# Keys first, identity turns during the loads, and an earlier place on ScalarE for two units' exponentials: one core of a Trainium2

## The chip, the cores and the metric

The kernel runs on one core of one Trainium2 chip. The metric is the device time of one execution in microseconds (us), and of several executions the median is taken. Everything is 32-bit float. The engines are named as in the profile: PE is TensorE's matmul, PEld its weight load, DVE is VectorE, ACT is ScalarE, POOL is GpSimd, SP is SyncE, which only issues DMAs here. ACT issues DMAs too, so there are two DMA queues.

## What is computed

```python
scores = (q @ k.T) / 8                      # 8 batch rows, 8 heads, 576 tokens, 64 wide
thresh = max(scores, axis=-1) - tau
scores = where(scores >= thresh, scores, -1e9)
attn   = exp(scores - max(scores))
attn   = attn / (sum(attn) + 1e-9)
x      = attn @ v                           # heads side by side: (8, 576, 512)
h      = relu(x.T @ w_tok1) @ w_tok2        # mixes the tokens, 576 -> 256 -> 576
u      = x + h.T
out    = u + relu(u @ w_ch1) @ w_ch2        # mixes the channels, 512 -> 1536 -> 512
```

The weights come as 64-bit floats and are turned into 32-bit floats on the chip.

## The kernel before

The work is cut into 144 units, 18 for each batch row. A unit is 128 query tokens of one pair of heads (one unit in nine shares its tokens between two pairs). The program order is written out by hand: one loop over `u` emits, for each `u`, the scores of unit `u` and the later steps of earlier units, and every engine runs its own instructions in the order in which they were emitted. The steps that matter here are these.

- `load_qk` loads one pair of heads. Queries (`lq`) and keys (`lk`) arrive in eight parts, four of queries (even numbers) and four of keys (odd numbers), each 32 columns wide; a list of two queues says which engine issues queries and which issues keys. For pair 0 the first 128 query tokens were loaded ahead of the other 448.
- `prep` turns the loaded blocks into `qT` and `kT` with DVE transposes (L286).
- `scores` (L304) puts the scores of a unit into two PSUM tiles `sc`, one for each head of the pair; DVE takes their maximum `mx` (L309), POOL makes the `bias` of it (L310). There are two `sc` tiles, and a third in row 0.
- `weigh` is ACT's part: two Prelu instructions (L319) read `sc` and write `e`, which frees the PSUM tiles for the next unit's scores, and two exponentials (L326) work in place on `e`. For two heads it is one block of four large instructions.
- `norm` divides `e` by its sum (DVE L333 and L334, POOL L337).
- `turn` is used in batch row 0 only. It transposes a unit's `e` on PE in three thirds of three 128x128 blocks (L355) into the PSUM tiles `tr`, of which there are two. The first and the last third are copied out by DVE and the middle third by ACT (all L357). From row 1 on `turn_blocks` does this with DVE and DMAs (L367). Turns run two units behind: units 16 and 17, row 0's last, are turned while units 18 and 19, row 1's first, are scored.
- `weight(n)` emits the next `n` steps of the conversion of the weights. A weight piece passes through ACT (L197, L199), DVE (L207, L209, L213) and POOL (L221), and L207 of a piece reads what L199 wrote.
- `fill` emits matmuls of the token and channel layers while the attention of later rows runs.
- `tau` is loaded by one small DMA on ACT's queue, and five DVE instructions of one column each (L620 to L624) make `toff` and `ntau` of it.

`weigh(u)` stood near the end of the loop body, behind `turn` and `weight`. In row 0 it was moved ahead of them in the iterations in which a group's values fall due (`visit`). In the two iterations that have a row-0 unit to turn while a row-1 unit is scored (`turns_left` is true, `u` = 18 and 19) it stood behind them.

A DMA issue waits, besides for its data, for the landing of an earlier DMA that used the same one of eight landing semaphores; the eight are handed out in turn.

Of the kernel before, what the change touches and what calls it, by code (L numbers as in the profile page):

```python
# [9 lines left out]
F32 = mybir.dt.float32  # L10
# [7 lines left out]
P = 128  # L18
# [3 lines left out]
def kernel(  # L22
# [25 lines left out]
    nc = tc.nc  # L48
    B, H, S, D = q.shape
# [5 lines left out]
    MAIN = NI * P  # L55
# [14 lines left out]
    work = ctx.enter_context(tc.tile_pool(name="work", bufs=2))  # L70
    small = ctx.enter_context(tc.tile_pool(name="small", bufs=6))
    ps_sc = ctx.enter_context(tc.tile_pool(name="ps_sc", bufs=2, space=bass.MemoryType.PSUM))
    ps_tr = ctx.enter_context(tc.tile_pool(name="ps_tr", bufs=2, space=bass.MemoryType.PSUM))
# [17 lines left out]
    loaded = {}  # L91
# [3 lines left out]
    def load_qk(n, eng, parts=range(8), blocks=(range(S // 32),) * 2):  # L95


        b, p = pairs[n]
        if n not in loaded:
            loaded[n] = [ld.tile([P, S // 32, 32], F32, tag=tag, bufs=1, name=f"{tag}_{n}") for tag in ("lq", "lk")]  # L100
        for part in parts:
            i, which = divmod(part, 2)
            h, c = divmod(i, 2)
            lo, hi = blocks[which].start, blocks[which].stop
            eng[which].dma_start(
                out=loaded[n][which][32 * i : 32 * i + 32, lo:hi],
                in_=(q, k)[which][b, 2 * p + h, 32 * lo : 32 * hi, 32 * c : 32 * c + 32].rearrange("(n t) d -> t n d", t=32),
            )
# [9 lines left out]
    ident = const.tile([P, P], F32, name="ident")  # L118
# [1 line left out]
    for t in vlast:  # L120
        nc.gpsimd.memset(t, 0.0)

    load_qk(0, (nc.sync, nc.scalar), blocks=(range(P // 32), range(S // 32)))
    load_qk(0, (nc.sync, None), range(0, 8, 2), blocks=(range(P // 32, S // 32), None))
    nc.scalar.dma_start(out=tau_sb, in_=bass.AP(tensor=tau.tensor, offset=0, ap=[[0, P], [1, 1]]))

    w1 = const.tile([P, NT, DTOK], F32, name="w1")
# [143 lines left out]
    heads = {}  # L271
# [5 lines left out]
    def in_blocks(b):  # L277
        return b > 0

    def prep(n, first=S // 32):  # L280

        srcs = loaded.pop(n)
        heads[n] = [work.tile([P, S], F32, tag=name, name=f"{name}_{n}") for name in ("qT", "kT")]
        for which, lo, hi in ((0, 0, first), (1, 0, S // 32), (0, first, S // 32)):
            if lo < hi:
                nc.vector.transpose(  # L286
                    out=heads[n][which][:, 32 * lo : 32 * hi], in_=srcs[which][:, lo:hi].rearrange("p n d -> p (n d)")
                )

    def scores(u):  # L290
        b, p0, t = units[u]
        sc = [
            (ps_3rd if b == 0 and (2 * u + h) % 3 == 2 else ps_sc).tile([P, 2, MAIN], F32, tag="sc", name=f"sc{h}_{u}") for h in range(2)
        ]
        if t == SHARED:
            parts = [(b * NP + p0, slice(MAIN, S), slice(0, 64)), (b * NP + p0 + 1, slice(0, LAST), slice(64, P))]
        else:
            o = P * t if t < SHARED else LAST + P * (t - SHARED - 1)
            parts = [(b * NP + p0 + (t > SHARED), slice(o, o + P), slice(0, P))]
        order = [(f, part, h) for f in range(2) for part in parts for h in range(2)]  # L300
        for f, (n, cols, rows), h in order if b else sorted(order, key=lambda o: o[2]):
            r = slice(D * h, D * h + D)
            qT, kT = heads[n]
            nc.tensor.matmul(sc[h][rows, f, 0:HS], lhsT=qT[r, cols], rhs=kT[r, HS * f : HS * f + HS], start=True, stop=True)  # L304
        mx = small.tile([P, 2], F32, tag="mx", name=f"mx_{u}")
        bias = small.tile([P, 2], F32, tag="bias", name=f"bias_{u}")
        for h in range(2):
            c = slice(h, h + 1)
            nc.vector.tensor_reduce(out=mx[:, c], in_=sc[h][:, :, 0:HS], axis=AX.XY, op=ALU.max)  # L309
            nc.gpsimd.tensor_scalar(out=bias[:, c], in0=mx[:, c], scalar1=toff, scalar2=-SCALE, op0=ALU.add, op1=ALU.mult)  # L310
        st[u] = sc, bias

    def weigh(u):
        sc, bias = st.pop(u)
        rs = small.tile([P, 2], F32, tag="rs", name=f"rs_{u}")
        e = work.tile([P, 2 * S], F32, tag="e", bufs=3, name=f"e_{u}")
        for h in range(2):
            eh = e[:, S * h : S * h + S].rearrange("p (f x) -> p f x", f=2)
            nc.scalar.activation(out=eh, in_=sc[h][:, :, 0:HS], func=AF.Prelu, bias=bias[:, h : h + 1], scale=SCALE, alpha=STEEP)  # L319
        st[u] = e, rs  # L320

        if b_now:
            fill(0.2)
        for h in range(2):
            eh = e[:, S * h : S * h + S]
            nc.scalar.activation(out=eh, in_=eh, func=AF.Exp, bias=ntau, accum_out=rs[:, h : h + 1])  # L326
            if b_now:
                fill(0.2)
# [259 lines left out]
    def fill(share):  # L588
        nonlocal credit
        credit += share * quota  # L590
        while todo and credit > 0:
            cost, step = todo.popleft()
            credit -= cost
            step()
        if not todo:
            credit = 0.0
# [19 lines left out]
            todo.extend(channel_mlp(b - b % 2, uT, i))  # L616
        quota = (sum(c for c, _ in todo) - (KEEP if b else KEEP_FIRST)) / (UB - 1)

    prep(0, P // 32)
    nc.vector.tensor_scalar(out=tlow, in0=tau_sb, scalar1=0.0, scalar2=-3.0e38, op0=ALU.is_lt, op1=ALU.mult)  # L620
    nc.vector.tensor_scalar(out=toff, in0=tau_sb, scalar1=0.0, scalar2=FAR, op0=ALU.max, op1=ALU.min)
    nc.vector.tensor_scalar(out=toff, in0=toff, scalar1=-1.0 / SCALE, scalar2=None, op0=ALU.mult)
    nc.vector.tensor_add(out=toff, in0=toff, in1=tlow)
    nc.vector.tensor_scalar(out=ntau, in0=toff, scalar1=SCALE, scalar2=None, op0=ALU.mult)  # L624
    due = deque()
    b_now = 0
    LAG = 2
# [13 lines left out]
    for u in range(len(units) + LAG + 4):  # L641
        on = u < len(units)
        if u == UB:
            late.close()
            ps_mm = ctx.enter_context(tc.tile_pool(name="ps_mm", bufs=2, space=bass.MemoryType.PSUM))
        if on:
            b_now, p0, t = units[u]
            n = b_now * NP + p0
        w = u - LAG
        back = 0 <= w < len(units)  # L650
        if on:
            scores(u)

        last = False
        visit = False
        if due and not in_blocks(due[0][1]):
            visit = due[0][0] <= u
            last = values_due(u)
        elif early:
            early.popleft()[1]()  # L660
        if 0 < u <= len(units):
            norm(u - 1)

        turns_left = b_now and back and not in_blocks(units[w][0])
        if b_now:
            if not turns_left:
                weight(2)
        else:


            weight_to(2.25 * (u - (1 if visit else 1.5)))
            if visit and on:
                weigh(u)
        while copies:
            copies.popleft()()
        if last and u < UB:
            early.extend(token_mlp(0, range(NP // 2))[0])
        elif last:
            push(0)
        if back:  # L680
            wb, wp, wt = units[w]
            if not in_blocks(wb):
                for i in range(3):
                    turn(w, i)
            if wt % GU == GU - 1:
                g = wt // GU
                if g < 2:
                    split_middle(wb * NP + wp + g)
                due.append((u + (2 if in_blocks(wb) else 1), wb, wp, g))
        if b_now:  # L690
            fill(0.4)
        if back and in_blocks(wb):
            turn_blocks(w)
        if b_now:
            weight(4 if turns_left else 2)
        if on and (b_now or not visit):
            weigh(u)
        elif b_now:
            fill(0.6)
        if b_now:  # L700
            weight(2)
        elif u == 0:
            on_scalar(0, 0)
            on_scalar(0, 1)
        else:
            weight_to(2.25 * (u - 1))
        if on:


            when = {3: (2, 0, 2), 4: (2, 2, 4), 5: (2, 4, 6), 6: (2, 6, 8), 8: (3, 0, 3), 0: (1, 3, 6), 1: (1, 6, 8)}  # L710
            if u == 0:
                load_qk(1, (nc.sync, nc.sync), range(0, 3))
            if t in when:
                m, lo, hi = when[t]
                if n + m < len(pairs):
                    load_qk(n + m, (nc.scalar if b_now else nc.sync,) * 2, range(lo, hi))
            if t in (3, 7) and n + 2 + t // 4 < len(pairs):
                load_v(n + 2 + t // 4)
            if t == 2:
                prep(n + 1)  # L720
            if t == 7 and n + 2 < len(pairs):
                prep(n + 2)
        if due and in_blocks(due[0][1]):
            values_due(u)

        if back and wt % GU == 0 or not on:
            move_u()
# [31 lines left out]
```

## Time and profile before

| | |
|---|---|
| median of 5 runs | 1354.25 us (1353.75 to 1356.04) |
| the profiled execution | 1354.09 us, of which its span is 1352.3 us |
| PE busy | 1304.9 us, 96% of the span |
| DVE, ACT, POOL busy | 44%, 43%, 26% |
| mean granted PE clock | 0.991 |
| first score matmul | 6.91 us into the span |
| first maximum (DVE L309) | 9.23 us |
| first Prelu (ACT L319) | 10.47 us |
| row 1's first unit scored | 98.87 us |

A profile line of the timeline reads: start in us, duration in us, engine, line, operation, what it writes `<-` what it reads, shapes, `xcount` of merged instructions, and in brackets how long its engine sat idle before it and what ended that. A line of the chain of work that ended last reads: start, length, what. A line of the table by stages gives, for a stretch `A:B`, its length, then each engine's busy time with the count of its instructions, then the granted PE clock (1 is full speed), the share of time in which the DMA engines were busy, and GB/s.

### The profile page before, as it was taken

The page shows a single profiled execution, that of the slowest core. Times are in us where ns is not written, and L with a number is a line of the kernel's source. Part 1 is how long each engine was busy: PE and PEld are TensorE (multiplying, and loading weights), DVE is VectorE, ACT ScalarE, POOL GpSimd, SP SyncE. Part 2 cuts the span into 40 slices and gives each one's busy share as a digit, 9 for nine tenths or more (in the row PEclk, how much of TensorE's full clock was granted, in tenths as well). Part 3 has the DMA queues.
Part 4 walks back from the last instruction along what each step waited for, and adds up shares of the span by engine and source line. Part 5 has one row for each costly group of instructions (what it writes and reads, how often), then busy time and mean ns, then how long its engine had stood idle before and what let it go on. Part 6 is the DMA issues. An engine that isn't in the chain of part 4 may idle for free.

```text
span 1352.3 us, 17840 instructions
## 1 busy us (share of the span) xinstructions
PE 1304.9 (96%) x6162; PEld 812.0 (60%) x6162; DVE 592.7 (44%) x1026; ACT 585.2 (43%) x1299; POOL 354.6 (26%) x683
## 2 busy tenths in 40 slices
PE   6888899999999999999999999999999999999999
PEld 4555656547474666565665567465657466575677
DVE  6878874435443444434344444435443454201000
ACT  6776664444444444443434444344434453120110
POOL 4565652222222222212122222222221222100000
PEclk8998999999999999999999999999999999999999
DMA  5434764545354444443445435534443453400000
GB/s 123 117 88 121 203 167 96 126 95 130 89 130 97 105 108 105 121 108 87 92 102 125 104 78 128 127 81 110 114 102 82 113 119 78 112 24 17 23 24 32
DMA packets 296746, 135.31 MB, mean 100 GB/s; under 512 B 204816, under 2 KB 289552, under 8 KB 296656
## 3 DMA queue, kind: packets, MB, share of 16 engines
q1 hardware_dynamic: 168048, 118.16, 34.4%
q10 hardware_dynamic: 128608, 16.01, 7.5%
q8 instruction: 49, 0.80, 0.2%
q14 instruction: 41, 0.34, 0.1%
HBM read 43.25 MB, written 9.44 MB: 39 GB/s over the span
## 4 chain that ended last, share of the span: by engine, by line
PE 89%; DVE 5%; ACT 2%; DMA 2%; issue 1%; POOL 1%; SPq 0%; ACTq 0%; DVEq 0%; POOLq 0%
PE c L528 27%; PE c L507 27%; PE sc L304 12%; PE pv L416 9%; PE t L454 5%; PE t L464 4%; PE pv L411 3%; DVE mx L309 2%; PE tx L447 1%; ACT e L319 1%; PE tr L355 1%; PE c_h L555 1%; DMA lk<-in_k_dram 1%; DMA lq<-in_q_dram 1%; ACT e L326 0%
## 5 line engine op out<-in xcount | busy, mean ns | idle before, releaser
L507 PE MATMUL c<-xT,wc 128*128 128x256 f32 (+1 forms) x1920 | 400.2, 362 | 0.1
L309 DVE TENSOR_REDUCE mx<-sc 128x1 f32<-128x576 f32 x288 | 204.2, 750 | 446.7 <-PE sc L304 446.7
L528 PE MATMUL c<-wc,g 128*128 128x512 f32 x840 | 379.0, 597 | 0.0
L507 PEld LDWEIGHTS c<-xT,wc 128*128 128x128 f32 x1920 | 334.5, 191 | 69.8 <-issue 29.7
L310 POOL TENSOR_SCALAR bias<-mx,toff 128x1 f32<-128x1 f32 x288 | 82.6, 287 | 775.6 <-DVE mx L309 720.9
L319 ACT ACTIVATE e<-sc,bias 128x576 f32<-128x576 f32 x288 | 199.8, 740 | 179.3 <-POOL bias L310 174.6
L528 PEld LDWEIGHTS c<-wc,g 128*128 128x128 f32 x840 | 154.4, 190 | 176.3 <-issue 172.9
L326 ACT ACTIVATE e<-e,ntau 128x576 f32<-128x576 f32 x288 | 221.1, 772 | 0.0
L337 POOL TENSOR_SCALAR e<-e,rr 128x576 f32<-128x576 f32 x288 | 214.7, 758 | 14.3 <-ACT g L508 2.6
L508 ACT ACTIVATE g<-c 128x256 f32<-128x256 f32 (+1 forms) x240 | 86.9, 362 | 297.0 <-PE c L507 273.4
L304 PE MATMUL sc<-kT,qT 64*128 64x288 f32 (+1 forms) x1280 | 192.5, 434 | 12.7 <-DVE kT L286 6.9
L367 DVE STREAM_TRANSPOSE T<-e 128x1152 f32<-128x1152 f32 x126 | 171.9, 1364 | 4.8 <-DMA eT<-T 2.6
L304 PEld LDWEIGHTS sc<-kT,qT 64*128 64x128 f32 (+1 forms) x1280 | 106.4, 178 | 98.7 <-issue 56.7
L416 PE MATMUL pv<-eT,lv 128*64 128x384 f32 (+1 forms) x1024 | 137.5, 409 | 0.0
L416 PEld LDWEIGHTS pv<-eT,lv 128*64 128x64 f32 x1024 | 75.5, 138 | 50.8 <-issue 42.5
L421 ACT COPY xT<-pv 128x384 f32<-128x384 f32 (+1 forms) x56 | 21.0, 400 | 166.8 <-PE pv L416 163.8
L464 PE MATMUL t<-w,a 128*128 128x288 f32 x256 | 75.1, 420 | 8.2 <-DVE xT L468 4.8
L540 DVE TENSOR_TENSOR us<-c,ut 128x512 f32<-128x512 f32 x26 | 17.9, 690 | 137.5 <-PE c L528 120.4
L454 PE MATMUL t<-x_sb,w 128*128 128x512 f32 (+1 forms) x180 | 73.6, 557 | 0.0
L464 PEld LDWEIGHTS t<-w,a 128*128 128x128 f32 x256 | 45.8, 191 | 30.3 <-issue 10.5
L468 DVE TENSOR_TENSOR xT<-xT,t 128x288 f32<-128x288 f32 x64 | 28.3, 446 | 71.1 <-PE t L464 70.6
L326 ACT ACTIVATION_READ_ACCUMULATOR e<-e,ntau 128x1 f32 x288 | 56.6, 197 | 0.0
(49 smaller groups left out, 562.6 us busy)
## 6 DMA issues: line engine op xcount, KB each, us to landing
eT<-T SPq DMA_DIRECT2D x672, 108.0 KB, 2.3
scratch<-in_moe_w_ch_dram SPq DMA_DIRECT2D x24, 512.0 KB, 3.7
lv<-in_v_dram SPq DMA_DIRECT2D x32, 288.0 KB, 3.3
out_dram<-us SPq DMA_DIRECT2D x35, 256.0 KB, 2.2
lk<-in_k_dram ACTq DMA_DIRECT2D x111, 72.0 KB, 2.6
lq<-in_q_dram ACTq DMA_DIRECT2D x106, 72.0 KB, 2.3
ut<-us SPq DMA_DIRECT2D x192, 32.0 KB, 1.9
lq<-in_q_dram SPq DMA_DIRECT2D x18, 72.0 KB, 3.4
```

The source lines that it names most:

```text
L304: nc.tensor.matmul(sc[h][rows, f, 0:HS], lhsT=qT[r, cols], rhs=kT[r, HS * f : HS * f + HS], start=True, stop=True)
L309: nc.vector.tensor_reduce(out=mx[:, c], in_=sc[h][:, :, 0:HS], axis=AX.XY, op=ALU.max)
L319: nc.scalar.activation(out=eh, in_=sc[h][:, :, 0:HS], func=AF.Prelu, bias=bias[:, h : h + 1], scale=SCALE, alpha=STEEP)
L326: nc.scalar.activation(out=eh, in_=eh, func=AF.Exp, bias=ntau, accum_out=rs[:, h : h + 1])
L337: nc.gpsimd.tensor_scalar(out=eh, in0=eh, scalar1=rr[:, h : h + 1], scalar2=1.0, op0=ALU.mult, op1=ALU.mult)
L367: nc.vector.transpose(out=T[:, :, place, :].rearrange("p a (c x) -> p c a x", c=NK), in_=e.rearrange("p (c a x) -> p c a x", c=NK, a=4))
L416: nc.tensor.matmul(to[r], lhsT=lv[:, j, :], rhs=e[j], start=False, stop=(c == NI - 1), skip_group_check=True)
L454: nc.tensor.matmul(to, lhsT=w1[:, t, P * m : P * m + P], rhs=x_sb[:, t, cols], start=(t == 0), stop=(t == NT - 1))
L464: nc.tensor.matmul(to, lhsT=a[:, m, P * c : P * c + P], rhs=w2[:, m, HS * f : HS * f + HS], start=(m == 0), stop=(m == NTK - 1))
L507: nc.tensor.matmul(ps, lhsT=wc1[:, j, c, :], rhs=uT[:, c, GR * i : GR * i + n], start=(c == 0), stop=(c == NCC - 1))
L508: nc.scalar.activation(out=s["g"][:, j, 0:n], in_=ps, func=AF.Relu)
L528: nc.tensor.matmul(flat, lhsT=s["g"][:, j, P * t : P * t + P], rhs=wc2[:, j, :], start=(j == 0 and b > 0), stop=(j == NJ - 1), skip_group_ ...
```

## The change

There are three edits.

1. The first loads. The four parts of the keys of pair 0 are now issued first, two by SP and two by ACT; then the four first parts of its queries (128 tokens), two by each; then, as before, SP alone issues the other 448 query tokens. `tau` stays behind them on ACT's queue. DVE's order at the start becomes: keys' transpose, first queries' transpose, the five `tau` instructions, the other queries' transpose. Before it was: first queries, keys, other queries, `tau`.
2. 24 PE transposes of the identity into a `tr` tile that nobody reads stand ahead of the first score matmul.
3. At `u` = 18 and 19 `weigh(u)` is emitted ahead of `turn` and `weight`. On ACT these two units' Prelus and exponentials come to stand ahead of the copy of the turn's middle third and ahead of one L197/L199 pair. The `fill` calls there have nothing to emit yet. PE, POOL and the later part of every other engine's order stay the same.

```diff
-    load_qk(0, (nc.sync, nc.scalar), blocks=(range(P // 32), range(S // 32)))
-    load_qk(0, (nc.sync, None), range(0, 8, 2), blocks=(range(P // 32, S // 32), None))
+    FIRST = P // 32
+    for which in (1, 0):
+        for i in range(2):
+            for eng, half in ((nc.sync, 0), (nc.scalar, 1)):
+                load_qk(0, (eng, eng), [2 * (2 * half + i) + which], (range(FIRST), range(S // 32)))
+    load_qk(0, (nc.sync, None), range(0, 8, 2), (range(FIRST, S // 32), None))
...
-    prep(0, P // 32)
+    warm = ps_tr.tile([P, MAIN], F32, tag="tr", name="warm")
+    for _ in range(24):
+        nc.tensor.transpose(out=warm[:, 0:P], in_=ident, identity=ident)
+    prep(0, ((1, 0, S // 32), (0, 0, FIRST)))
     nc.vector.tensor_scalar(out=tlow, in0=tau_sb, ...)
...
+    prep(0, ((0, FIRST, S // 32),))
...
         turns_left = b_now and back and not in_blocks(units[w][0])
         if b_now:
-            if not turns_left:
+            if turns_left:
+                weigh(u)
+            else:
                 weight(2)
         else:
             weight_to(2.25 * (u - (1 if visit else 1.5)))
-            if visit and on:
+            if visit:
                 weigh(u)
...
         if b_now:
             weight(4 if turns_left else 2)
-        if on and (b_now or not visit):
+        if turns_left:
+            fill(0.6)
+        elif on and (b_now or not visit):
             weigh(u)
```

`prep` takes the list of pieces to transpose in place of one number; for all later pairs it emits what it did before.

More of the change, by code (lines that the diff above doesn't have):

```diff
@@ L278, in in_blocks, with prep @@
         return b > 0
[L280 to L288, printed above, removed]
+    def prep(n, parts=((0, 0, S // 32), (1, 0, S // 32))):
+        if n not in heads:
+            heads[n] = [work.tile([P, S], F32, tag=name, name=f"{name}_{n}") for name in ("qT", "kT")]
+        for which, lo, hi in parts:
+            nc.vector.transpose(
+                out=heads[n][which][:, 32 * lo : 32 * hi], in_=loaded[n][which][:, lo:hi].rearrange("p n d -> p (n d)")
+            )
     def scores(u):
```

## The prediction

> **What bounds the kernel now.** I read the page's chain of work first, to see what a microsecond saved at the start is worth.
>
> ```profile
> PE 89%; DVE 5%; ACT 2%; DMA 2%; issue 1%; POOL 1%; SPq 0%; ACTq 0%; DVEq 0%; POOLq 0%
> ```
>
> PE is 89% of it; the rest is where other engines or loads hold PE up. The change touches only two such places, 0 to 24 us and 98 to 124 us. Behind each lies PE work of fixed amount, so a gain or loss there should reach the end whole. The chain from 0 to 24 us, its longest pieces:
>
> ```profile
> 1.17 2.07 DMA lq<-in_q_dram
> 3.27 2.73 DMA lk<-in_k_dram
> 6.07 0.79 DVE kT L286
> 6.91 2.30 PE sc L304 x8
> 9.23 0.77 DVE mx L309
> 10.47 1.37 ACT e L319 x2
> 11.85 1.51 ACT e L326 x4
> ...
> 15.13 2.29 PE sc L304 x4
> 17.41 1.49 PE tr L355 x6
> 19.45 0.92 PE tr L355 x3
> ```
>
> The keys' last part is issued only at 3.27, when a queries' part has landed, and lands at 6.00. Then come kT, unit 0's scores, maximum, Prelu and exponentials, each waiting for the one before. Now the same stretch by the clock:
>
> ```profile
> 6.90:11.00 4.10, 4.09 (x12) 2.54 (x12) 2.63 (x8) 0.53 (x1) 0.52 (x2) 1.00 1.07 347
> 14.00:17.50 3.50, 2.37 (x5) 1.32 (x6) 0.46 (x2) 3.22 (x7) 1.63 (x3) 0.52 0.81 129
> 17.50:21.00 3.50, 2.93 (x13) 2.07 (x15) 2.34 (x7) 2.08 (x4) 1.99 (x3) 0.50 0.01 1
> 21.00:24.40 3.40, 3.06 (x14) 1.76 (x10) 3.37 (x8) 2.60 (x7) 0.54 (x2) 0.50 0.00 0
> 24.40:28.00 3.60, 2.63 (x25) 1.74 (x25) 3.60 (x7) 3.60 (x9) 3.60 (x5) 1.00 0.00 0
> ```
>
> The clock is at half from 14 to 24 us. The 1.00 of the first row can't be right: eight score matmuls take 2.30 us at 6.91, and 1.24 us at 36.05 (`36.05 1.24 PE sc L304 x8` in the chain), so unit 0 ran at half speed too. Last, the second place, from the timelines of ACT and DVE:
>
> ```profile
> 104.14 0.39 ACT L456 ACTIVATE a<-t 128x256 f32<-128x256 f32 x1 [5.09 <-PE t L454]
> 104.80 0.48 ACT L357 COPY eT<-tr 128x384 f32<-128x384 f32 x1 [0.27 <-PE tr L355]
> 106.28 1.36 ACT L319 ACTIVATE e<-sc,bias 128x576 f32<-128x576 f32 x2
> ```
> ```profile
> 107.67 0.42 DVE L207 TENSOR_SCALAR high<-high 128x512 f32<-128x512 f32 x1
> 108.12 1.39 DVE L209 TENSOR_SCALAR wc<-high 128x512 uint32<-128x512 uint32 x1
> 110.16 1.42 DVE L309 TENSOR_REDUCE mx<-sc 128x1 f32<-128x576 f32 x2
> ```
>
> Unit 18's Prelus start at 106.28, though their bias was there at 102.46 and ACT was idle until 104.14. But the chain there runs through DVE: L207, L209, L213, then unit 19's maximum.
>
> **Keys first.** Issues on a queue stand 0.48 us apart at the start (SP's eight in 3.85 us). Two keys' parts on each queue are issued at 0.73 and 1.2, the queries' firsts at 1.65 and 2.1, none of them behind a landing. Parts of keys took 2.1 to 2.7 us to land, so they land at 2.8 to 3.9; queries' firsts took 2.0, so 4.1. kT (0.78) and the first of qT (0.31) then end near 5.0. Before, kT ended at 6.85: PE's data are ready 1.9 us earlier. The queries' rest and the first weight piece go out some 0.4 us later on SP; that piece, 5.4 us from issue to landing, would be there near 10.4, and ACT's L197 needs it only at 13.25, or about 12 after this change, so it costs nothing.
>
> **The turns of the identity.** At half clock six turns take 1.54 us (17.34) and three 0.90 (19.45): (1.54 - 0.90) / 3 = 0.213 us each. At full clock 0.87 (26.39) and 0.55 (28.08): 0.107 each. The identity is ready at 1.30, so 24 turns end between 1.35 + 24 x 0.107 = 3.9 and 1.35 + 24 x 0.213 = 6.5. PE is in order, so unit 0's scores start at 5.0 at best and 6.5 at worst. With 1.24 or 2.30 us each they end between 6.3 and 8.8, against 9.21.
> Whether turns raise the clock: in the row 21.00:24.40 PE is busy 3.06 us, of which 1.54 are six turns, and the clock then rises; in 14.00:17.50, with 2.37 us busy and nearly all of that scores, it didn't. So turns seem to count, and I take the clock to rise while they run or soon after, in mid range: scores end near 7.5. [...]
>
> **The `tau` steps in DVE's way.** They now stand ahead of the rest of qT, and unit 0's maximum stands behind both. `tau` is issued when the first keys' part lands (near 3.0) and took 3.3 us to land, so 6.3; with 2.1, 5.1. Five instructions took 0.75 (8.22 to 8.97): done by 5.9 to 7.1. The other queries' last part waits for a queries' first (4.1) and is issued at 4.4; with the median landing of 2.5 it is there at 6.9, with the 3.5 of the same part before at 7.9. Its transpose takes 0.65: DVE is free at 7.55 to 8.55, which also holds unit 1's scores. The first maximum starts at the later of scores and DVE: from 7.55 to 8.8, I take 8.0. Against 9.23 the gain is 1.2 (0.4 to 1.7). The tile that the turns write is one of the two `tr` tiles; they are long over when row 0's first turns need it (17.34), so that costs nothing. From there ACT works almost without a gap to 17 us, so its start carries the stage.
>
> **The clock afterwards.** PE was idle from 13.1 to 15.1, because unit 2's second head waits for unit 1's Prelu. That gap stays, and shorter scores before it make more gaps; I take the clock to fall again. If it doesn't, 15.13 and 17.41 and 19.45 shrink by 1.05, 0.62 and 0.37, in all 2.0.
>
> **Units 18 and 19.** Nothing is added; ACT's order changes. Prelus of unit 18 start at about 104.5 in place of 106.28, and unit 19's scores, which wait for their PSUM tiles, at 105.65 (after the last third's turns) in place of 107.06. That is 1.4 us for PE, but not for DVE. Behind ACT's block of 2.77 us (106.28 to 109.05) now queue the middle third's copy (0.38) and L197/L199 (1.1): L199 ends near 108.8, not 106.38. DVE's L207 needs it: 108.85 in place of 107.67, and behind L207 queue L209, L213, unit 19's maximum and the copy that lets unit 17's last turns go. Part of this is covered: L209 took 1.39 at 108.12 while POOL's L221 ran (107.83 to 109.23), and 0.43 at 106.60. Starting after L221 it saves 0.96. So 1.2 - 0.96 = 0.24 late, 0.4 if L207 too is slowed. The last turns and unit 20's scores (113.2) follow: +0.3. In unit 19 the same L207 comes at 116.3, its L199 now near 116.0: nothing. The middle copy of unit 17, near 114.9, is ahead of the value matmuls (115.90). Bounds: -1.4 if DVE keeps pace, +1.2 if L209 saves nothing.
>
> **Sum.** -1.2 + 0.3 = -0.9 on the profiled execution's 1354.09 (0.16 below the median): 1353.2.
>
> **Rivals.**
> *The early clock holds.* If no stretch before 15 us is empty enough, the 2.0 come on top: 1351.2. For it: PE starts 5.6 us earlier. Against: the gaps above. 0.15.
> *The turns bring nothing.* They run at half clock and the scores after them too, so the first maximum starts at 8.8: -0.4 + 0.3, 1354.0. For it: the half clock of unit 0, and the turns outlasting the data. 0.18.
> *Units 18 and 19 cost more, and it is slower.* L207 waits its full 1.2 us, and PE, done early with unit 19's scores and unit 17's first turns, is idle from 109.3 to 113 in one piece where it had 1.4 and 2.0. The clock was at half from 113.2 to 120 in the trace; one more stretch of 3.4 us at half costs 1.7. Together +2.9; less the start's 1.2, 1355.8, or 1356.6 with a start of -0.4. It decides as soon as L199's delay exceeds what L209 gains, about 1 us. 0.12.
> My forecast, a start between these two, has 0.55; its own bounds are 1352.7 to 1354.0.
>
> **How the numbers follow.** The runs spread 2.3 us, and 0.2%, 2.7 us, is about what a measurement here can tell from no change: below 1351.5 or above 1357.0. Below lies most of the first rival and the tail of the forecast: 0.16. Above lies only the far end of the third: 0.06. Within: 0.78. The range reaches from the first rival with the best start (-1.7 - 2.0 + 0.3: 1350.7) to the third's first figure: 1350.7 to 1355.8. What is left out is the far half of the third, some 0.06, and clock phases that I can't place, some 0.1.
>
> **What would show it.** Right: first score at 5 to 6.5, first maximum at 7.6 to 8.8, first Prelu 0.4 to 1.7 earlier; at unit 18 Prelus 1.7 earlier, but L207 late with ACT L199 as its releaser, and unit 20's scores no earlier than before relative to unit 18's. Wrong: a first maximum before 7.5, a clock that stays full past 15, or unit 20's scores over 1 us earlier or later relative to unit 18's.

## The result and the profile after

The changed kernel's median is 1352.31 us (24 runs, 1350.66 to 1355.28), against 1354.72 us (44 runs, 1351.45 to 1358.43) for the kernel before on the same chips. The ratio is 0.9985, with a 95% interval of 0.998 to 0.9991: 2.0 us faster (1.2 to 2.7); the two medians are 2.4 us apart. The forecast was 1353.2 us, 0.9 us faster, in a range of 1350.7 to 1355.8. So the time lies in the range and on the forecast side, within the 0.2% that the prediction named as about what a measurement here can tell from no change, and the gain is about twice the one worked out. Twelve more sets of runs, two of them repeats of the kernels before and after, were made to see which part of the change brings it.

The lines of the code have moved: scores are L306 (L304 before), `mx` L311, Prelu L321, exponential L328, turns L357, their copies L359, the weight steps L201, L203 (ACT) and L211, L213, L217 (DVE), the turns of the identity L624.

The changed kernel's chain of work that ended last, its shares and then its first 24 us. The columns of a piece are start, length, what; SPq is the time that SP takes to issue a DMA.

```profile
PE 85%; DVE 6%; DMA 3%; ACT 2%; issue 1%; POOL 1%; SPq 1%; ACTq 0%; DVEq 0%; POOLq 0%
```
```profile
1.18 3.02 DMA lk<-in_k_dram
...
4.21 0.31 SPq L105
...
4.57 0.48 SPq L105
...
5.09 2.90 DMA lq<-in_q_dram
...
8.12 0.65 DVE qT L288
8.76 0.65 DVE mx L311
...
9.89 1.37 ACT e L321 x2
...
14.54 2.29 PE sc L306 x4
16.83 1.49 PE tr L357 x6
```

Before, the chain ran through the keys and PE (`kT`, then eight score matmuls). In this execution no PE work stands in it until 14.5 us. The keys' last part lands at 4.20, and that landing lets SP issue the second of the four parts of the other 448 query tokens, at 4.21; the third goes out at 4.57 and the last at 5.09, which lands near 8.0, is transposed, and only then DVE is free for unit 0's maximum. The first Prelu comes at 9.89, 0.58 us earlier than the 10.47 of before. Unit 2's second half (14.54) has the same 0.6.

A second profiled execution of the same kernel (`after_again` below) has another chain. There the queries' rest is transposed by 7.71 (7.06 + 0.65), and the turns, which end at 6.74, hold up the scores and with them the maximum:

```profile
1.35 5.38 PE warm L624 x24
6.74 1.22 PE sc L306 x8
...
7.98 0.77 DVE mx L311
```

PE's timeline of the first execution, with the idle time before an instruction and what ended it in brackets:

```profile
1.35 5.37 PE L624 MATMUL warm<-ident 128*128 128x128 f32 x24 [1.35 <-POOL ident masks.py:199]
6.66 1.25 PE L306 MATMUL sc<-kT,qT 64*128 64x288 f32 x8
8.82 1.24 PE L306 MATMUL sc<-kT,qT 64*128 64x288 f32 x4 [0.91 <-DVE qT L288]
```

The 24 turns take 5.37 us, 0.22 each, and unit 0's eight score matmuls 1.25 us, the full-clock figure (2.30 before). They are done at 7.91, but DVE is not free before 8.7. The clock rose only at 6.59, when the turns were all but over, so they ran at half clock and held the scores, whose data were ready at 5.51, until 6.66. Then the table by stages, in the rows of which the prediction spoke:

```profile
14.00:17.50 3.50, 2.96 (x8) 1.91 (x9) 0.63 (x1) 2.63 (x6) 1.05 (x3) 0.50 0.98 157
17.50:21.00 3.50, 2.93 (x13) 1.94 (x13) 2.34 (x8) 2.66 (x6) 1.99 (x3) 0.50 0.06 9
21.00:24.40 3.40, 2.83 (x15) 1.62 (x11) 3.37 (x8) 2.61 (x6) 1.12 (x3) 0.61 0.00 0
24.40:28.00 3.60, 2.77 (x28) 1.76 (x26) 3.57 (x9) 3.55 (x9) 3.45 (x6) 1.00 0.02 5
```

The clock falls again (at 13.42) and is back at 23.66. It does so in the kernel before too, at 14.17 and 24.41. Last, units 18 and 19 from the timelines of ACT, DVE and PE:

```profile
104.00 1.37 ACT L321 ACTIVATE e<-sc,bias 128x576 f32<-128x576 f32 x2
...
106.76 0.48 ACT L359 COPY eT<-tr 128x384 f32<-128x384 f32 x1
107.12 0.71 ACT L201 ACTIVATE scratch<-scratch 128x512 int32<-128x512 uint32 x1
...
107.69 0.70 ACT L203 ACTIVATE high<-scratch 128x512 f32<-128x512 f32 x1
```
```profile
108.42 0.57 DVE L211 TENSOR_SCALAR high<-high 128x512 f32<-128x512 f32 x1 [1.10 <-ACT high L203]
109.03 0.43 DVE L213 TENSOR_SCALAR wc<-high 128x512 uint32<-128x512 uint32 x1
109.49 0.69 DVE L217 SCALAR_TENSOR_TENSOR wc<-scratch,wc 128x512 uint32<-128x512 uint32 x1
110.10 1.42 DVE L311 TENSOR_REDUCE mx<-sc 128x1 f32<-128x576 f32 x2
```
```profile
112.66 0.90 PE L357 MATMUL tr<-ident,e 128*128 128x128 f32 x3 [4.18 <-DVE eT L359]
113.49 2.29 PE L306 MATMUL sc<-kT,qT 64*128 64x288 f32 x8
```

Unit 18's Prelus come at 104.00 in place of 106.28. ACT's block then holds the copy and the pair L201/L203; DVE waits 1.10 us for L203; L213 costs 0.43 in place of 1.39; and unit 19's maximum starts at 110.10, as before (110.16). PE, which had its part done earlier, is idle for 4.18 us in one piece, and unit 20's scores start at 113.49 (113.20 before). All that ACT gained is gone at that point; what follows until unit 21 is taken up with the prediction's account.

### The profile page after: what moved, and what is told of

The parts are those of the page before. It is cut to its first block, busy times and chain, and to the rows that moved or that the text cites. A ratio compares the mean times of both kernels' runs of the same rounds, so it can differ in the third digit from the quotient of the medians.

```text
span 1349.8 us, 17890 instructions
## 1 busy us (share of the span) xinstructions
PE 1306.5 (97%) x6186; PEld 815.1 (60%) x6186; DVE 591.7 (44%) x1026; ACT 585.5 (43%) x1299; POOL 354.4 (26%) x683
## 4 chain that ended last, share of the span: by engine, by line
PE 85%; DVE 6%; DMA 3%; ACT 2%; issue 1%; POOL 1%; SPq 1%; ACTq 0%; DVEq 0%; POOLq 0%
PE c L530 26%; PE c L509 26%; PE sc L306 11%; PE pv L418 8%; PE t L456 5%; PE t L466 4%; PE pv L413 3%; DVE mx L311 2%; PE tx L449 1%; DMA lk<-in_k_dram 1%; ACT e L321 1%; DMA scratch<-in_moe_w_ch_dram 1%; PE tr L357 1%; DVE high L211 1%; PE c_h L557 1%
## 5 line engine op out<-in xcount | busy, mean ns | idle before, releaser
L311 DVE TENSOR_REDUCE mx<-sc 128x1 f32<-128x576 f32 x288 | 204.2, 750 | 445.4 <-PE sc L306 444.2
L321 ACT ACTIVATE e<-sc,bias 128x576 f32<-128x576 f32 x288 | 200.0, 741 | 182.7 <-POOL bias L312 177.3
L328 ACT ACTIVATE e<-e,ntau 128x576 f32<-128x576 f32 x288 | 221.1, 772 | 0.0
L306 PE MATMUL sc<-kT,qT 64*128 64x288 f32 (+1 forms) x1280 | 190.3, 432 | 6.4 <-ACT e L321 5.5
L306 PEld LDWEIGHTS sc<-kT,qT 64*128 64x128 f32 (+1 forms) x1280 | 104.9, 178 | 92.1 <-issue 56.9
L328 ACT ACTIVATION_READ_ACCUMULATOR e<-e,ntau 128x1 f32 x288 | 56.7, 197 | 0.0
```

## The experiments

Each kernel was compared with the kernel before on the same chip. "First maximum" is the start of DVE's first `mx` in the one profiled execution. Times are medians. The ratio and its interval are those of the comparison on record; they are not the quotient of the two medians, which differs from them by up to 0.0008 (keys_only: 1352.62 / 1353.95 = 0.9990), so differences of a microsecond between two rows carry little.

| kernel | this, us | before, us | ratio (95%) | first maximum, us |
|---|---|---|---|---|
| changed kernel | 1352.31 | 1354.72 | 0.9985 (0.998 to 0.9991) | 8.69 |
| start_only (edits 1, 2) | 1352.15 | 1353.95 | 0.9982 (0.9971 to 0.9994) | 8.11 |
| units_only (edit 3) | 1353.55 | 1353.95 | 0.9997 (0.9987 to 1.0007) | 8.98 |
| turns_only (edit 2) | 1354.04 | 1353.95 | 1.0 (0.9988 to 1.0012) | 8.66 |
| keys_only (edit 1) | 1352.62 | 1353.95 | 0.9982 (0.997 to 0.9995) | 7.81 |
| before_again | 1353.74 | 1354.21 | 0.9999 (0.9989 to 1.001) | 8.94 |
| rest_both | 1353.12 | 1354.21 | 0.9992 (0.9983 to 1.0) | 9.03 |
| conv_first | 1353.06 | 1354.21 | 0.9991 (0.9982 to 1.0) | 8.76 |
| keep_clock | 1352.46 | 1354.21 | 0.9992 (0.998 to 1.0004) | 7.97 |
| after_again | 1351.97 | 1354.38 | 0.9978 (0.9968 to 0.9988) | 7.98 |
| keys_units (edits 1, 3) | 1351.25 | 1354.38 | 0.9983 (0.9971 to 0.9994) | 8.31 |
| keys_again (edit 1) | 1352.74 | 1354.38 | 0.9987 (0.9978 to 0.9996) | 7.87 |
| keys_conv18 | 1350.79 | 1354.38 | 0.9973 (0.9964 to 0.9983) | 8.41 |

### Which edit brings the gain: four kernels on one chip

**start_only**: the change without edit 3.

```diff
         if b_now:
-            if turns_left:
-                weigh(u)
-            else:
+            if not turns_left:
                 weight(2)
...
-        if turns_left:
-            fill(0.6)
-        elif on and (b_now or not visit):
+        if on and (b_now or not visit):
             weigh(u)
```

> The first two edits alone (keys first, turns of the identity); units 18 and 19 as in the kernel before. Theory 1, the start is worth what the first maximum gains and no more: first maximum at 8.7 us as in the changed kernel (9.23 before), every maximum of units 2 to 5 earlier by 0.58 us, unit 20's scores 0.1 to 0.6 us earlier than the 113.20 of before, time 0.3 to 0.8 us below the kernel before (ratio 0.9994 to 0.9998). Rival, the shift of the start also changes what later stages wait for, and the whole gain of 2 us hangs on it: ratio 0.998 to 0.999.

Measured: 0.9982, in the rival's band and not in the theory's. The gain of the whole change is there without edit 3. The interval, 0.8 to 3.9 us, still holds the 1.12 us by which this profile's first maximum comes earlier.

**units_only**: the kernel before with edit 3 alone (the diff above, the other way round).

> The third edit alone (units 18 and 19's Prelus and exponentials ahead of the turns); the start as before. Theory 1, DVE's L207 waits for ACT's L199 in unit 18 for about 1.1 us and eats the earlier scores: Prelu of unit 18 some 1.8 us earlier than the 106.28 of before, first maximum of unit 19 within 0.5 us of 110.16, unit 20's scores 0.3 to 0.8 us later than 113.20, time 0.3 to 0.8 us above the kernel before (ratio 1.0002 to 1.0006). Rival, the edit saves what PE does between unit 20's scores and unit 21's maximum (the clock's half period there was 3.4 us shorter in the changed kernel's profile): unit 21's first maximum 1 us or more ahead of 129.61, ratio 0.998 to 0.9993.

Measured: 0.9997, no change that can be told. The interval allows anything from 1.8 us faster to 0.9 us slower. Its DVE timeline has the wait of the changed kernel, by the line numbers of before:

```profile
108.49 0.57 DVE L207 TENSOR_SCALAR high<-high 128x512 f32<-128x512 f32 x1 [1.09 <-ACT high L199]
```

From the start of unit 18's maxima to that of unit 20's scores it is 13.22 us (100.23 to 113.45), against 12.53 (100.67 to 113.20) before: 0.7 later, where the prediction had 0.3. In the changed kernel it is 12.92 (100.57 to 113.49), 0.4 later. But unit 21's first maximum stands at 128.50, 1.1 us ahead of the 129.61 of before, as the rival had it: behind unit 20's scores the half-clock stretch is 3.41 us long here and 6.83 before.

**turns_only**: the kernel before with the 24 turns, in the old order of loads.

```diff
+    warm = ps_tr.tile([P, MAIN], F32, tag="tr", name="warm")
+    for _ in range(24):
+        nc.tensor.transpose(out=warm[:, 0:P], in_=ident, identity=ident)
     prep(0, P // 32)
```

> The 24 turns of the identity alone, with the loads in the order of before. Theory 1, turns of the identity raise the clock by themselves: half clock and 5.1 us of turns, then unit 0's scores at 6.9 us take 1.25 us and not 2.30, but DVE still has the queries' rest and the tau steps to do until 8.97, so the first maximum comes at 9.0 (0.2 us earlier), ratio 0.9997 to 1.0000. Rival, turns don't count as activity for the clock: scores 2.30 us long, first maximum at 9.23, no gain at all.

Measured: 1.0. The turns do raise the clock (at 6.26, with nothing else on PE), unit 0 is scored in 1.25 us, and the first maximum comes at 8.66, against a mean of 9.05 in the three other profiles with the old order (9.23, 8.94, 8.98). Nothing of that 0.4 can be seen in the time.

**keys_only**: edit 1 alone; the changed kernel without edit 3 and without the turns.

```diff
-    warm = ps_tr.tile([P, MAIN], F32, tag="tr", name="warm")
-    for _ in range(24):
-        nc.tensor.transpose(out=warm[:, 0:P], in_=ident, identity=ident)
     prep(0, ((1, 0, S // 32), (0, 0, FIRST)))
```

> The new order of the first loads and of DVE's first steps alone, without turns of the identity and without the edit of units 18 and 19. Theory 1, the queries' rest decides: unit 0's scores start at 5.6 us and run at half clock until 7.9, which is still ahead of DVE, whose transpose of the queries' rest ends at 8.7; the first maximum stands at 8.7 as with the turns, and the time is that of the start alone. Rival, the clock decides: unit 1's scores, 8.8 to 11.0 at half clock in place of 8.8 to 10.1, hold up unit 1's maxima and from there the Prelus, and the maxima of units 2 to 5 are only 0 to 0.3 us earlier than before.

Measured: 0.9982, the same as with the turns. Its DVE and PE timelines:

```profile
4.26 0.78 DVE L288 STREAM_TRANSPOSE kT<-lk 128x576 f32<-128x576 f32 x1 [4.26 <-DMA lk<-in_k_dram]
5.12 0.31 DVE L288 STREAM_TRANSPOSE qT<-lq 128x128 f32<-128x128 f32 x1
7.15 0.65 DVE L288 STREAM_TRANSPOSE qT<-lq 128x448 f32<-128x448 f32 x1 [0.48 <-DMA lq<-in_q_dram]
7.81 1.42 DVE L311 TENSOR_REDUCE mx<-sc 128x1 f32<-128x576 f32 x2
```
```profile
5.49 5.83 PE L306 MATMUL sc<-kT,qT 64*128 64x288 f32 x15 [5.49 <-DVE qT L288]
```

PE starts its scores at 5.49, works at half speed (the first record of the clock is a rise at 22.36) and is still not late: its eight scores end at 7.79 (5.49 + 2.30) and the transpose of the queries' rest at 7.80, and the maximum follows. At half clock for the whole start it has the earliest first maximum of all kernels. So the early clock is no part of what the start gains.

### What holds the first maximum

**rest_both**: the changed kernel, with the queries' other 448 tokens issued by both queues, and `tau` right behind the keys.

```diff
+        if which == 1:
+            nc.scalar.dma_start(out=tau_sb, ...)
-    load_qk(0, (nc.sync, None), range(0, 8, 2), (range(FIRST, S // 32), None))
-    nc.scalar.dma_start(out=tau_sb, ...)
+    for i in range(2):
+        for eng, half in ((nc.sync, 0), (nc.scalar, 1)):
+            load_qk(0, (eng, eng), [2 * (2 * half + i)], (range(FIRST, S // 32), None))
```

> The changed kernel with one more edit of the first loads: the other 448 query tokens are issued by both queues, two parts each, and tau goes out right behind the keys. Theory 1, the first maximum waits for the transpose of these queries and nothing else: their transpose starts at 6.9 to 7.4 us (8.12 in the changed kernel), and the first maximum at 7.6 to 8.0, where the scores at full clock end (7.9); 0.5 to 1.0 us less than the changed kernel, ratio to the kernel before 0.9975 to 0.9985. Rival, the DMA engines are what is full, not the queues that issue: the last part lands at 8.0 again, the first maximum stays at 8.1 to 8.7, and the time is that of the changed kernel.

Measured: 0.9992, and the first maximum at 9.03, the latest with the new order. The chain of this kernel:

```profile
1.78 3.21 DMA tau_sb<-in_tau_dram
4.98 0.02 issue
5.00 3.33 DMA lq<-in_q_dram
```

The last part is issued at 5.00, as in the changed kernel (5.09), because now the issue waits for the landing of `tau`. Two queues did not bring it forward, and its landing took 3.33 us, against 2.90. Whether more parts under way made it longer, as the rival has it, is not separated here. Which of the waits for a landing semaphore could be freed without making another one was not tried further.

**before_again**: the kernel before, unchanged.

> The kernel before, unedited, as a second look at it and as a measure of what two sets of runs of one kernel differ by. Theory 1, the landing of the first loads and the phase of the clock's periods differ from execution to execution: the first maximum stands within 0.3 us of 9.23, but the half-clock periods lie elsewhere and later maxima differ from the first look by up to 2.5 us; ratio 1.000 within 0.0012. Rival, two executions run alike: all maxima up to unit 20 within 0.2 us of the first look.

Measured: 0.9999, and its first maximum 0.29 earlier than in the first profile, at 8.94. Two executions of one kernel differ by 0.3 at 9 us and by 1.2 at unit 36 (242 us). A single profile therefore settles no difference of half a microsecond, and the first maxima were compared in groups: with the new order of loads nine profiles (all with it but rest_both) have 7.81 to 8.76, mean 8.21; with the old order four have 8.66 to 9.23, mean 8.95. With the turns the mean of the new order is 8.30 (five profiles), without them 8.10 (four); the old order without turns has 9.05 (three). So both edits together bring 0.75 us there, and the new order without turns 0.95.

### The second place: units 18 and 19

**conv_first**: the changed kernel, with three steps of the weights' conversion ahead of the Prelus at `u` = 18 and 19, so that DVE's L211 doesn't wait for a late L203.

```diff
             if turns_left:
+                weight(3)
                 weigh(u)
...
-            weight(4 if turns_left else 2)
+            weight(1 if turns_left else 2)
```

> The changed kernel, but in units 18 and 19 three of the weight conversion steps are emitted ahead of the unit's Prelus, so that L207 no longer waits behind them and DVE does its part while it would be idle. Theory 1, that wait is what ate the gain of the earlier scores: no idle time of DVE ahead of L207 in unit 18, first maximum of unit 19 at 107.3 to 108.0 (110.10 in the changed kernel), unit 20's scores 1 to 2 us earlier than 113.49; 0.5 to 1.5 us less than the changed kernel. Rival, another wait takes its place at once (PE's turns behind the copies, or the weight pieces' loads): unit 20's scores within 0.4 us of 113.49.

Measured: 0.9991. The wait is gone, and from unit 18's maxima to unit 19's it is 7.78 us (101.53 to 109.31) in place of 9.53 in the changed kernel. But another wait takes its place. DVE's timeline:

```profile
109.31 1.41 DVE L311 TENSOR_REDUCE mx<-sc 128x1 f32<-128x576 f32 x2
...
111.28 0.41 DVE L211 TENSOR_SCALAR high<-high 128x512 f32<-128x512 f32 x1
111.73 0.86 DVE L213 TENSOR_SCALAR wc<-high 128x512 uint32<-128x512 uint32 x1
112.62 1.11 DVE L217 SCALAR_TENSOR_TENSOR wc<-scratch,wc 128x512 uint32<-128x512 uint32 x1
113.65 0.54 DVE L359 COPY eT<-tr 128x384 f32<-128x384 f32 x1
```

In the second of the two iterations the three steps now stand on DVE ahead of unit 17's copy, which comes at 113.65 (112.07 in the changed kernel); unit 20's scores start at 115.08, 13.55 us behind unit 18's maxima where the changed kernel has 12.92.

**keep_clock**: the changed kernel, with 36 more turns of the identity in the gap between unit 17's second and last third.

```diff
                 for i in range(3):
                     turn(w, i)
+                    if i == 1 and w == UB - 1:
+                        idle = ps_mm.tile([P, DM], F32, tag="mm", name="idle")
+                        for _ in range(36):
+                            nc.tensor.transpose(out=idle[:, 0:P], in_=ident, identity=ident)
```

> The changed kernel with 36 more turns of the identity on PE between unit 17's second and last third, where PE was idle from 108.5 to 112.7 us. Theory 1, turns count as activity, so the clock does not fall there: no half-clock period begins between 110 and 117 us, and unit 21's first maximum comes 9.0 to 10.0 us after unit 20's (9.5 in the changed kernel, 10.8 before); up to 1.7 us less for each 3.4 us at half clock avoided. Rival, the clock falls because of the waits before and after, turns or not: a half-clock period begins there as in every look so far, and the turns only delay unit 17's last third by up to 0.5 us.

Measured: 0.9992. PE's timeline, and the row of the table by stages in which the changed kernel's clock is 0.50:

```profile
108.56 4.09 PE L698 MATMUL idle<-ident 128*128 128x128 f32 x36
112.91 0.55 PE L357 MATMUL tr<-ident,e 128*128 128x128 f32 x3 [0.25 <-DVE eT L359]
113.39 1.24 PE L306 MATMUL sc<-kT,qT 64*128 64x288 f32 x8
...
122.33 0.88 PE L466 MATMUL t<-w,a 128*128 128x288 f32 x2 [1.92 <-DVE xT L470]
```
```profile
112.40:115.80 3.40, 2.95 (x20) 1.50 (x20) 2.73 (x5) 3.40 (x8) 2.95 (x3) 1.00 0.00 1
```

With the gap filled the clock stays full and unit 20's scores take 1.24 us in place of 2.29. The gain is given back nine microseconds later, where PE waits 1.92 us for DVE, and a half-clock stretch follows that wait (122.83 to 126.24). Unit 21's maxima come 10.75 us after unit 20's, where the theory had 9.0 to 10.0 and the changed kernel has 9.48. The stretch was moved, not removed.

### The last four, on one chip

**after_again**: the changed kernel once more.

> The changed kernel once more, as the measure for the other three of this group. If its first comparison (about 2.0 us faster) was not a matter of one chip, its ratio lies between 0.998 and 0.9995 again. First maximum between 8.0 and 8.8 us (mean of five kernels with the new order of loads so far: 8.27), half clock from 110 to 117 us in one stretch of 3.41 us, unit 20's scores near 113.5.

Measured: 0.9978 (0.9968 to 0.9988), a little below the expected band. The gain is not a matter of one chip, and by the interval it is at least 1.6 us on this one.

**keys_units**: the changed kernel without its turns (the diff of keys_only's).

> The changed kernel without its 24 turns of the identity. Theory: the turns bring nothing and the load order brings all of the start; then the first maximum stands at 7.6 to 8.3, the first record of the clock is a rise later than 18 us, and the time is that of the changed kernel or up to 1 us less. Rival (the turns do pay once unit 1 is scored at full clock): unit 1's scores and maxima 0.4 us later than in the changed kernel against the same first maximum, and the time 0.5 to 1 us above it.

Measured: 0.9983, median 0.7 us below after_again and mean 0.2 below, with 9 and 11 runs whose standard deviation is 1.7 and 1.1 us: no difference. In the profile unit 1's first maximum does come 1.1 us later behind unit 0's than in the changed kernel (2.46 where it has 1.40), as the rival said, since PE is at half clock; by unit 2's second head that is gone. The turns are worth nothing that these runs can see.

**keys_again**: edit 1 alone, once more.

> The load order alone once more. It measured 0.9982 (0.997 to 0.9995) on another chip, with the first maximum at 7.81. Theory (what the start gains is about 0.7 to 1 us and the rest of that figure was spread): ratio between 0.9988 and 0.9998, first maximum between 7.6 and 8.4. Rival (the gain is really over 2 us and arises later than the start): ratio at or below 0.9985, with a gain over 2 us already standing in the maxima of units 30 to 60.

Measured: 0.9987 (0.9978 to 0.9996), between the two expectations, the first maximum at 7.87. The rival's second condition, over 2 us in units 30 to 60, does not hold at unit 30 (1.3) and holds at unit 38 (3.1), so neither is settled.

**keys_conv18**: keys_units, with the three steps ahead of the Prelus at `u` = 18 alone.

```diff
             if turns_left:
+                if u == UB:
+                    weight(3)
                 weigh(u)
...
-            weight(4 if turns_left else 2)
+            weight((1 if u == UB else 4) if turns_left else 2)
```

> As the kernel without turns, and at unit 18 alone three steps of the conversion stand ahead of the Prelus (at unit 19 none do, as in the changed kernel). Theory (the wait of DVE L211 for ACT L203 held unit 19's maximum): unit 18's Prelus are 1.1 us later than in the changed kernel, L211 does not wait, unit 19's maximum comes near 109 in place of 110.1 and unit 20's scores 0.5 to 1.5 us earlier than 113.5; the time is 0 to 1.5 us below the kernel without turns. Rival (another wait takes its place, as when both units had the steps ahead): unit 17's last copy on DVE or unit 19's own Prelus come no earlier, unit 20's scores stay within 0.4 of 113.5, and the time is the same within 0.5 us.

Measured: 0.9973 (0.9964 to 0.9983), the lowest time of all. DVE and PE:

```profile
105.10 0.57 DVE L211 TENSOR_SCALAR high<-high 128x512 f32<-128x512 f32 x1
105.71 1.40 DVE L213 TENSOR_SCALAR wc<-high 128x512 uint32<-128x512 uint32 x1
107.14 0.69 DVE L217 SCALAR_TENSOR_TENSOR wc<-scratch,wc 128x512 uint32<-128x512 uint32 x1
107.75 1.42 DVE L311 TENSOR_REDUCE mx<-sc 128x1 f32<-128x576 f32 x2
...
110.96 0.56 DVE L359 COPY eT<-tr 128x384 f32<-128x384 f32 x1 [0.70 <-PE tr L357]
```
```profile
110.31 0.61 PE L357 MATMUL tr<-ident,e 128*128 128x128 f32 x3 [2.19 <-DVE eT L359]
110.85 2.29 PE L306 MATMUL sc<-kT,qT 64*128 64x288 f32 x8
```

L211 has no wait in front of it any more, though L213 now takes its slow 1.40 us. From unit 18's maxima to unit 20's scores it is 10.90 us (99.95 to 110.85); in keys_units it is 12.25 (101.08 to 113.33). That is 1.35 us less, and PE's idle time is 2.19 in place of 4.37. Unit 18's Prelus stand 3.69 us behind its maxima, 1.1 later than in keys_units (2.58). The changed kernel, whose clock was at half from 98.75 to 102.17, has 3.43 there, so the expectation's 1.1 held against the one and not the other. Against after_again the median is 1.2 us lower, against keys_units, from which it differs by these steps alone, 0.5 us. The intervals against the kernel before overlap, so the version has the lowest time measured, but that it is faster than keys_units is not shown.

## Why the prediction was right, and where its size was off

**The chain.** The places were read rightly: the gain comes with the first (edits 1 and 2: 0.9982), and the second alone gives nothing that can be told (0.9997). That a gain there reaches the end whole is not borne out by the profiles. The changed kernel's first profile leads that of before by 0.58 us at unit 5's first maximum (29.84 against 30.42) and by 0.16 at unit 6's (37.16 against 37.32). The lines are those of unit 6, first before, then after:

```profile
37.32 1.42 DVE L309 TENSOR_REDUCE mx<-sc 128x1 f32<-128x576 f32 x2 [0.68 <-PE sc L304]
```
```profile
37.16 1.42 DVE L311 TENSOR_REDUCE mx<-sc 128x1 f32<-128x576 f32 x2 [1.09 <-PE tr L357]
```

After the change this maximum waits for three turns that PE does behind its scores. All ten profiles with edit 1 have this wait (1.08 to 1.10 us), none of the four without it does (0.68). The prediction had no such term, and why the maximum waits there is not shown. In start_only, whose clock came back late, the lead goes from 1.13 us at unit 3 to 0.02 at unit 4.

**Keys first.** Predicted: keys there at 2.8 to 3.9, data ready at 5.0. Measured: the last keys' part landed at 4.20, `kT` began at 4.40, and the data were ready at 5.51 (5.20 + 0.31); in the four profiles without turns PE begins at 5.36 to 5.54. The step that was off is the landing time: four keys' parts at once took up to 3.02 us, where the parts of before took 2.1 to 2.7.

**The turns.** 0.213 us each at half clock was right (0.224), and so was the end at 6.5 as the latest (scores from 6.66). That they raise the clock was right too, but the rise came at 6.59, not in mid range, so the scores ended at 7.91 and not at 7.5. That it matters was wrong: in the first profile DVE set the maximum alone, and in after_again and keep_clock, where the scores set it (7.98 and 7.97, after 0.27 and 0.26 us of idle DVE), it was because the turns held them until 6.7. The rival that they bring nothing had the verdict on the turns (turns_only 1.0) and the wrong reason: in keys_only slow scores do not delay the maximum.

**`tau` and the queries' rest.** This is the term that was mis-sized. The other queries' last part was to be issued at 4.4; it was issued at 5.09, because SP issued the four parts one after another (3.10, 4.21, 4.57 and 5.09): the second waited for the keys' landing at 4.20, and it and the third took 0.31 and 0.48 us to issue. With a landing of 2.90 (2.5 to 3.5 predicted) DVE was free at 8.7, beyond the 8.55 given as the late end. So the start's gain was 0.54 in the first maximum of this profile and 0.75 in the mean of the groups, not 1.2; both lie in the stated bounds of 0.4 to 1.7. `tau`'s five instructions (5.83 to 6.61) ended long before and cost nothing.

**The clock afterwards.** It fell at 13.42, in the predicted stretch of 13 to 15, and no kernel in which it had risen by then kept it past 14.2. The rival that the early clock holds falls.

**Units 18 and 19.** Each step shows in the trace: Prelus 2.2 us earlier behind unit 18's maxima (104.00 - 100.57 in place of 106.28 - 100.67; predicted 1.8), L211 held by L203 (108.42; predicted 108.85), L213 down to 0.43, unit 20's scores later by 0.4 to 0.7 (predicted 0.3). The rival that made it slower had the long idle stretch of PE right (4.18 us in one piece), but not the clock: half clock lasted 3.41 us here and 6.83 before. The account must not stop at unit 20's scores: against unit 18's maxima, unit 21's come 1.07 us earlier than before in the changed kernel (27.87 against 28.94) and 0.66 in units_only (28.28). Whether edit 3 shortens the stretch is open: with it, keep_clock aside, five of seven profiles have 3.41 us there; without it one of six has (keys_only), four have 6.83, and start_only has two pieces of 3.41. By the times edit 3 is worth nothing between start_only and the changed kernel (0.9982 and 0.9985) and 1.5 us between the medians of keys_again and keys_units, so a gain of about a microsecond is neither shown nor excluded. In keep_clock, which moved the stretch, nothing was won.

**The sum.** -0.9 was the forecast, and the runs give -2.0 (-2.7 to -1.2), and -2.4 in after_again's medians. The start measured 0.75, so 0.5 to 2 us of the gain are not in any term of the sum. The six comparisons that have edit 1, and beside it at most edits 2 and 3, lie at 0.9978 to 0.9987, the three without it at 0.9997 to 1.0, so the gain comes with edit 1. Its size is less sure: rest_both, conv_first and keep_clock, which have edit 1 and one further edit each, lie at 0.9991 and 0.9992, about 1.2 us. They are all from one chip, on which edit 1 was not run without a further edit, so whether their edits or the chip take the other microsecond is open. Where the gain arises stays open too. In the profiles the lead shrinks and grows by 1 to 3 us after unit 6, at places that differ between executions of the same kernel: in the changed kernel's first profile the lead is 0.14 us at unit 16 (86.38 against 86.52), 1.28 at unit 36 (241.55 against 242.82) and 2.92 at unit 38 (258.69 against 261.61); after_again is 0.24 behind at unit 16 and 0.17 ahead at unit 38. Two things do this in the traces: where half-clock stretches fall, and how long the value matmuls wait for landings between 222 and 262 us (4.2 us in all in the kernel before, 1.8 in the changed kernel's first profile, 2.9 in after_again). Neither was shown to be steered by the order of the first loads.

## What to carry to other kernels

When a load order is changed, follow the last part of the second load as closely as the first: here PE's data were there some 1.3 us earlier (5.4 to 5.5 in place of 6.6 to 6.9) and the first maximum came 0.75 earlier, because the engine that reads the scores stood in line behind the rest of the queries. Before such a gain is put into a sum, look at what the next units wait for: 0.4 us of it were gone at unit 6. Moving work ahead on one engine pays only as far as nothing that another engine needs is pushed back by it; the version that kept the three conversion steps ahead of the Prelus in one iteration, and behind them in the other, won 1.4 us there in its one profile, while doing it in both gave the gain to a new wait. The warmed clock was worth nothing here that the times show: where DVE set the end of the stretch it could not matter, and the 24 turns that raised it held the scores beyond the arrival of their data, by 1.15 us in the changed kernel's first profile (5.51 to 6.66) and by 1.35 in its second (5.32 to 6.67).

## What the runs showed of the hardware

- Turns of the identity, 32-bit here, raised PE's clock. In all seven profiles with the turns the first record of the clock is a rise, at 4.26 to 7.04 us, with nothing but turns on PE until at most 0.4 us before it; without turns the first rise stands at 10.24 to 10.76 in the old order and at 21.92 to 23.29 in the new.
- The half-clock stretches in these profiles lasted multiples of 3.41 us: 3.41, 6.83, 10.24 (13.42 to 23.66), 13.65 (13.61 to 27.26 in after_again) and 17.07 (11.09 to 28.16 in conv_first), but for the last one of a profile, which the end cuts (2.13 us in the first profile of before).
- How early the clock rose did not say how early the stage was over. In five of the seven profiles with turns the clock, having fallen, came back only at 27.25 to 28.43, and unit 4's maxima then lost 1.1 us of their lead against unit 3's; the four profiles without turns and with the new order lost nothing there. In the two pairs that differ by the turns alone the medians differ by 0.5 us in favour of the turns (start_only and keys_only) and by 0.7 us against them (after_again and keys_units), so this loss is not seen at the end.
- The mean granted clock was no measure of such things here: keys_only is cold for its first 22 us, and its rows there read 1.00, since the rate before the first record is not known to the profile. The same row shows that a busy PE alone did not raise the clock here: PE is busy for 5.45 of 5.60 us, and the first rise comes at 22.36, while in the kernel before it came at 10.76, after 4.09 us of the 4.10 in the row 6.90:11.00:

```profile
5.40:11.00 5.60, 5.45 (x16) 3.39 (x18) 3.53 (x10) 1.95 (x4) 0.53 (x2) 1.00 0.97 257
```

- The same DVE instruction, L213 on 128x512, took 0.43 us (109.03 in the changed kernel, POOL idle from 108.71 to 110.95) or 1.40 us (105.71 in keys_conv18, where POOL's L225 ran from 104.10 to 106.82). The prediction had counted on this, from two instances, and it held.
